# Linear attention and a feed-forward part in one kernel: last tokens of two heads in one tile, three weight differences on VectorE, stores on SyncE

## The chip, the cores and the metric

The kernel runs on one core of a Trainium2 chip, which has eight. The time is that of one execution of the whole program in device microseconds (us). A core has TensorE (PE in the profile; PEld is its weight loads), VectorE (DVE), ScalarE (ACT), GpSimd (POOL) and SyncE (SP), each with a queue of its own that it works off in order, and 16 DMA engines. A DMA is issued from the queue of SyncE, ScalarE or GpSimd.

## The reference

```python
def phi(x):
    proj = np.einsum('bhsd,df->bhsf', x, w_phi)
    proj = proj - np.max(np.abs(proj), axis=-1, keepdims=True)
    return np.concatenate([np.exp(proj), np.exp(-proj)], axis=-1)
q_p, k_p = phi(q), phi(k)                         # (8, 8, 576, 256)
kv = np.einsum('bhsf,bhsd->bhfd', k_p, v)
z = np.sum(k_p, axis=2)
num = np.einsum('bhsf,bhfd->bhsd', q_p, kv)
den = np.einsum('bhsf,bhf->bhs', q_p, z)[..., None] + 1e-06
x = (num / den).transpose(0, 2, 1, 3).reshape(4608, 512)
h = np.maximum(np.maximum(x @ w1, x @ w2), x @ w3)
return h @ w_out
```

There are 8 batches of 8 heads, 576 tokens and 64 elements a head; `w_phi` is 64 x 128, w1, w2 and w3 are 512 x 768, `w_out` is 768 x 512. Inputs and output are float32.

## The kernel before, in words

Attention runs in 16 **units**, each four heads of one batch. A unit's 576 tokens are 512 and the last 64, because a tile has 128 rows: a head has four full tiles of q and half a tile, so the half tiles are special throughout. A unit passes these stages, whose kinds are the names of nodes in the code:

- loads: `Lq` and `Lk` from GpSimd (they turn float32 into bf16), `Lv` (v) and `Lt` (the last tokens of q, `tail_raw`) from SyncE; `C` copies the last tokens beside k in `qk_bf`.
- `T` turns q and k so that the head's elements lie across the rows (`qkT`): on TensorE with a copy (`Tc`) for units 0 to 3, by a DMA transpose from SyncE for the others.
- `G` projects with `w_phi`; VectorE takes the largest absolute value (`rk`, `rq`), ScalarE the exponentials of k (`ek`); `M` projects q the other way round, with `eq` for its exponentials `Eq`.
- `E` makes the row factors `em` of k, GpSimd multiplies v by them (`va`, written to `vab`, whose last column is the factor itself, `vd`), and `K` multiplies by `Ek` (`kvps`, copied to `kv_sb`).
- `N` makes the numerators and, in column 65, the denominators: one product per tile and sign g of the exponent (`psn`). VectorE scales the one sign by `sq` (`xu`), adds the other (`xw`) and inverts the denominators (`xr`, `rden`); GpSimd divides (`x`, into `x_sb`).
- `X` turns x into `xT`: on TensorE with a copy for units 0 and 1, by a DMA transpose from SyncE for the others.

The feed-forward part runs in 9 **chunks** of 512 tokens: chunk b takes the first 512 tokens of all heads of batch b, that is the units 2b and 2b+1, and chunk 8 takes the last 64 tokens of all batches, which GpSimd gathers from `xT` (function `last`). The maximum of three products is rewritten: with the differences w2 - w1 and w3 - w1 (six nodes `wd`, each 256 columns of one matrix, made in place in `w_bf`), the kernel needs only max(0, x(w2 - w1), x(w3 - w1)), and x w1 w_out comes back as one product of x with a matrix that it makes once (`wt`, `we`, `wm`, `mo`; `lc` copies it later). So a chunk has 12 groups `up` into `ups`, evacuated by `t1` (relu) and `h` (maximum), then four groups `straight` and `down` into `ops`, a copy `osb`, and a store.

Every step is a node with its engine and the things that it waits for. **What sets the order** is a table, `PLAN`, of some 1,560 words such as `1201T4@37.6`: node, letter of the engine, buffers, and a start by which the words of one engine are put in order. Code reads the table and emits nodes in that order; on the chip an engine then goes as its semaphores let it. While n.start is below `WARM`, TensorE gets products of a constant (`idler`) in its gaps.

Of the kernel before, what the change touches and what calls it, by code (L numbers as in the profile page):

```python
# [8 lines left out]
FP32 = mybir.dt.float32  # L9
BF16 = mybir.dt.bfloat16  # L10
# [22 lines left out]
XW = SM + P  # L33
# [4 lines left out]
BY_HALF = 0  # L38
BY_BATCH = 99
# [10 lines left out]
TRAW = 2  # L50
WD_PE = 0
# [37 lines left out]
9G0@1.2 10S0@0.8 3A@1.1 1D@0.8 2G@1.9 16S0@1.3 0G@2.1 103G1@2.7 104G@7.2 4A@1.8 12D@4.0 8G@7.5 6D@4.2 11A@4.0  # L89
19T0@4.5 5A@4.3 7A@4.6 20D0@5.2 25T1@5.8 187S1@2.9 13S@4.5 26D@6.4 29T23@6.3 102G@8.2 30A0@6.7 51T45@6.9 73T67@7.1 110T0@8.0  # L90
105S1@5.1 34A0@7.2 106T1@8.1 18S2@5.7 53D0@7.3 33A@7.7 32D0@7.9 35D@8.5 107D1@9.1 119T53@9.9 75A0@8.2 31A@8.7 260G2@8.9 77A@9.1
74A0@9.6 186G3@9.6 259G@10.4 111D@9.7 76A@10.1 112T21@10.1 188G@11.1 124A1@10.6 123A1@11.1 126T06@10.3 52D@9.9 128A@11.5 17G@11.3 122D1@10.5
115D@11.1 127A@11.8 1166G@11.5 15D@11.7 27T4@12.1 14D@12.0 117A@12.1 120A@12.5 121A@13.0 1167G@12.3 1169G@13.0 130D1@12.2 28D@12.5 43T76@12.8
21T4@13.0 261G@13.8 129D@12.7 46D@13.1 47D@13.5 54A0@13.6 113A@13.8 78T0@13.3 22D@13.8 36T56@14.3 118D@14.1 125D@14.7 56G0@14.0 44A@14.3
114A@14.5 79A@15.0 23T4@14.6 39D@15.3 40A@15.3 24D@15.9 42D@16.3 48T23@16.4 55G@15.1 137A1@15.8 139G1@16.2 80A@16.0 45A@16.2 50D@16.9
116A@16.5 185G@17.3 58A@17.0 108T4@16.7 37A@17.2 334S0@11.6 140G@18.0 263T0@17.2 57A@17.7 59G@18.2 60G@19.3 267T7@17.7 68T13@17.9 61G@20.4
38A@17.8 49D@17.5 81A0@18.3 109D@18.1 264D2@18.7 268D@19.3 41A@18.5 72A@18.9 71A@19.4 138G@20.5 141A@19.9 131T25@18.8 142G@21.6 144A@20.1
62T46@19.1 64A0@20.2 69A@20.3 63A@20.8 70A@21.0 134T07@19.7 132D@19.5 190T3@20.1 65T26@20.6 1168G@22.7 133D@20.1 156T54@21.2 135D@20.7 82T01@21.6
67A@21.4 66A@21.6 161T6@21.9 136D@21.3 158A1@21.7 191D3@21.8 85T27@22.1 159A1@22.2 143G@23.4 83D0@22.4 160A@22.7 86D@22.9 333G0@24.5 157A@23.2
84D@23.3 164A1@23.7 265T3@22.6 163A@23.9 87D@23.7 332G@25.2 162A@24.1 145T04@23.4 146A1@24.4 151T21@23.9 147A@24.5 194T5@24.3 266D@24.1 155A@24.7  # L100
152A@25.2 195D@24.7 1180T7@24.4 93T60@24.8 153A@25.6 88D0@24.9 89G0@26.0 1181D0@25.0 1172G@27.6 90T34@25.1 154A@26.1 94D1@25.6 148T57@25.7 149A@26.6
91D@26.0 283T62@26.3 1178T3@26.5 165T15@27.0 285A0@26.7 284A0@27.0 95D@26.4 92D@26.8 1176T0@27.3 150A@27.3 287D0@27.2 96D1@27.5 1179A@27.4 168T47@27.7
97G@29.7 286D0@27.6 335G@30.9 196T26@28.1 98T3@28.5 166D2@28.0 1177A@28.3 169D@28.4 200A1@29.2 198A1@29.7 176T14@28.9 197A@30.1 167D@28.8 170D@29.2
276T50@29.4 177D0@29.6 99D@30.0 277A@30.6 173T71@30.1 178D@30.4 100T3@31.0 171D2@30.8 202D1@30.9 1170G@31.1 174D@31.5 278A@31.1 281A@31.6 199D@31.9
280A@32.1 175D@32.5 172G1@33.2 1186T4@31.4 1184T7@32.7 192T2@34.0 279D@32.9 210T15@34.6 179D0@33.5 403G1@34.4 337S0@38.0 189S3@39.4 101A@32.5 1187A@33.1
180G@35.1 201A@33.6 203T34@34.7 1185A@34.2 282D@33.6 208A@35.1 1171G@36.3 1173G@38.4 205A@35.6 262S0@40.0 214D1@34.9 269T60@34.9 270A@36.1 274A@36.5
181T7@35.2 1182T5@35.5 1183A@37.0 193D@35.2 183T2@36.8 473S1@40.6 182D@35.8 209D@36.2 204A@37.5 1188T7@37.1 272D@36.8 184D@37.4 213D@37.8 206D@38.1
271A@38.0 1189A@38.6 1194T5@38.4 207A@39.0 301T26@39.3 212A@39.5 275D@38.7 1175G@40.5 294A0@39.8 402G@42.6 1174G@43.3 221A1@40.0 224A0@40.2 305A0@40.3
288T37@39.6 304A0@40.8 303A@41.2 211A@41.7 1195D1@39.4 338S@42.2 336S2@43.9 297A1@42.0 1202T4@39.9 273A@42.1 302A@42.6 404G@45.4 289D@40.0 223G@45.7
612S0@45.8 290D@40.6 1200T5@40.7 1196T3@41.6 222G@47.7 1203D@41.2 291T76@42.6 228T41@42.8 229A1@43.2 1201D@41.8 1197D@42.7 230A1@43.7 218T50@43.0 293D@43.3  # L110
1206T2@43.3 238T3@44.2 1192T6@44.3 220D@43.9 232A@44.2 219D@44.5 406S1@47.4 1207D@45.1 239A@44.6 240A@44.9 1193A@45.4 215T40@45.3 306T53@45.5 292D@45.7
231A@45.8 216D@46.2 217D@46.8 1214T2@45.8 1204T6@46.7 1215D@47.4 310A@46.3 1205D@48.0 307A@46.8 309A@47.3 475S1@50.0 1198T7@47.5 241A0@47.7 339T14@48.5
# [12 lines left out]
541G@69.6 1226A3@71.3 395D@71.2 610G@70.3 386D@71.6 397D@72.0 485T64@71.8 490A1@72.2 545S2@67.5 492T03@72.0 496D1@72.4 750G2@71.0 398D@72.7 399D2@73.3
# [817 lines left out]
```

## Time and profile before

| | |
|---|---|
| median of the runs shown (3) | 281.54 us (281.24 to 284.22) |
| the profiled execution's own time | 282.56 us |
| its span, first to last instruction | 280.8 us |
| granted TensorE clock | 1.000 |
| DMA | 44.52 MB, mean 159 GB/s |
| engines, busy | PE 96%, DVE 77%, ACT 71%, POOL 58% |

A share of busy time is a mean over stages; matmuls are pipelined, so a busy TensorE is not one at its peak. Times in the rows below are microseconds from the first instruction of the span, and L with a number is a line of the kernel before.

### The profile page before, as it was taken

To read this page: it belongs to the slowest core of one execution; us is meant where nothing else is said; L and a number is where in the kernel's file an instruction comes from. 1 tells how busy PE (TensorE), PEld (TensorE's weight loads), DVE (VectorE), ACT (ScalarE), POOL (GpSimd) and SP (SyncE) were. 2 spreads that over 40 slices of the span, in tenths; PEclk is the share of its full clock that TensorE was granted. 3 is DMA by queue.
4 is the path that set the end of the run, shared out by engine and by line. 5 is a ranking of instruction groups with operands and counts; after the bars stand their busy time and mean duration, and the time that the engine had idled before them with its cause. 6 is when DMAs were issued, how large, how long until landed. Compare 5 with 4: busy or idle time off the path is not lost. (4 is left out here: it accounts for less than half of the span.)

```text
span 280.8 us, 8401 instructions
## 1 busy us (share of the span) xinstructions
PE 268.3 (96%) x3409; PEld 150.8 (54%) x3447; DVE 217.3 (77%) x442; ACT 199.1 (71%) x489; POOL 161.5 (58%) x161
## 2 busy tenths in 40 slices
PE   8789899999999999999999999999999999999993
PEld 5457654576655555555555456655546544444441
DVE  2799989999999969889997899898876871157320
ACT  4799999999999787698978879989589200310001
POOL 4879999998949703897336848393495341000000
PEclk9999999999999999999999999999999999999999
DMA  7999999997999999999999997717130224110253
GB/s 136 300 202 208 207 173 310 260 164 132 171 186 249 236 196 281 169 171 144 189 263 204 188 276 125 151 55 170 39 86 3 77 47 121 40 75 0 82 144 112
DMA packets 76214, 44.52 MB, mean 159 GB/s; under 512 B 52688, under 2 KB 67344, under 8 KB 76176
## 3 DMA queue, kind: packets, MB, share of 16 engines
q1 hardware_dynamic: 59536, 29.21, 49.8%
q0 software_dynamic: 14912, 11.77, 28.7%
q10 hardware_dynamic: 1728, 3.02, 3.0%
q8 instruction: 27, 0.44, 0.7%
q14 instruction: 11, 0.09, 0.1%
HBM read 34.64 MB, written 9.44 MB: 157 GB/s over the span
## 5 line engine op out<-in xcount | busy, mean ns | idle before, releaser
L748 PE MATMUL ups<-xT,w_bf 128*128 128x512 bf16 x414 | 101.3, 379 | 1.0
L584 ACT ACTIVATE Eq<-psm 128x512 bf16<-128x512 f32 (+1 forms) x160 | 81.7, 587 | 5.4 <-PE psm L593 3.1
L548 POOL TENSOR_TENSOR vab<-v_raw,em 128x1152 bf16<-128x1152 f32 (+1 forms) x36 | 68.2, 1907 | 22.9 <-ACT em L542 15.0
L504 ACT ACTIVATE Ek<-psk 128x512 bf16<-128x512 f32 x128 | 72.1, 633 | 8.2 <-PE psk L496 6.3
L748 PEld LDWEIGHTS <-w_bf 128*128 128x128 bf16 x432 | 39.2, 98 | 43.9 <-issue 2.3
L690 POOL TENSOR_TENSOR x_sb<-y,rden 128x640 bf16<-128x640 f32 x32 | 39.9, 1256 | 39.5 <-DVE rden L689 39.0
L786 PE MATMUL ops<-wout_bf,hT 128*128 128x512 bf16 (+2 forms) x214 | 50.5, 373 | 0.3
L758 DVE TENSOR_TENSOR hT<-hT,ups 128x512 bf16<-128x512 bf16 x54 | 35.5, 677 | 13.3 <-PE ups L748 11.1
L500 DVE TENSOR_REDUCE mq<-psq 128x4 f32<-128x512 f32 x64 | 41.2, 682 | 3.5 <-PE psq L496 3.2
L500 DVE TENSOR_REDUCE mk<-psk 128x4 f32<-128x512 f32 x64 | 41.9, 679 | 2.1 <-PE psk L496 1.7
L762 ACT ACTIVATE hT<-ups 128x512 bf16<-128x512 f32 x36 | 21.9, 620 | 24.5 <-PE ups L748 24.4
L641 DVE TENSOR_TENSOR y<-psn,sq 128x325 f32<-128x325 f32 x64 | 30.4, 491 | 6.7 <-PE psn L632 4.3
L796 ACT COPY osb<-ops 128x512 f32<-128x512 f32 x20 | 12.2, 608 | 32.3 <-PE ops L786 31.8
L786 PEld LDWEIGHTS <-hT 128*128 128x128 bf16 x222 | 20.6, 98 | 22.5 <-issue 0.2
L632 PEld LDWEIGHTS <-Eq 128*128 128x128 bf16 x640 | 26.3, 98 | 10.3 <-issue 0.4
L644 DVE TENSOR_TENSOR y<-y,psn 128x325 f32<-128x325 f32 x64 | 29.7, 487 | 1.6
L632 PE MATMUL psn<-kv_sb,Eq 128*128 128x65 bf16 x640 | 28.8, 194 | 0.2
L496 PEld LDWEIGHTS <-qkT 64*128 64x128 bf16 x576 | 18.0, 94 | 13.4 <-issue 8.3
L781 PE MATMUL ops<-xT 128*128 128x512 bf16 x87 | 23.7, 380 | 0.5
L567 PE MATMUL kvps<-vab,Ek 64*128 64x65 bf16 x1152 | 22.1, 191 | 0.8 <-POOL vab L548 0.6
L567 PEld LDWEIGHTS <-Ek 64*128 64x128 bf16 x1152 | 20.3, 94 | 3.4 <-issue 1.3
L796 DVE COPY osb<-ops 128x512 f32<-128x512 f32 (+2 forms) x17 | 11.1, 657 | 12.5 <-PE ops L786 12.5
(65 smaller groups left out, 263.9 us busy)
## 6 DMA issues: line engine op xcount, KB each, us to landing
v_raw<-in_v_dram SPq DMA_DIRECT2D x15, 576.0 KB, 6.0
out_dram<-osb SPq DMA_DIRECT2D x23, 256.0 KB, 3.3
qk_bf<-in_k_dram POOLq DMA_DIRECT2D x15, 288.0 KB, 6.9
qk_bf<-in_q_dram POOLq DMA_DIRECT2D x15, 256.0 KB, 8.7
w_bf<-in_moe_w_dram POOLq DMA_DIRECT2D x3, 768.0 KB, 13.2
out_dram<-osb ACTq DMA_DIRECT2D x9, 256.0 KB, 3.4
tail_raw<-in_q_dram SPq DMA_DIRECT2D x16, 64.0 KB, 4.8
wout_bf<-in_moe_w_out_dram POOLq DMA_DIRECT2D x1, 768.0 KB, 19.2
```

The source lines that it names most:

```text
L500: return nd(kind, {"DVE": 0.598 if n == 4 else 0.331}, lambda: nc.vector.tensor_reduce(dst(m()), ps()[:, 0:n, :], AXX, ALU.max, apply_abso ...
L504: return nd("ek", {"ACT": 0.478 if n == 4 else 0.264}, lambda: nc.scalar.activation(dst(Ek[g]()), ps()[:, 0:n, :], EXP, scale=1.0 - 2.0 * ...
L548: made.append(chosen(n_, lambda n_, g=g, t0=t0, t1=t1: (nc.vector if n_.eng == "DVE" else nc.gpsimd).tensor_tensor(vab()[:, g, t0:t1, 0:D] ...
L567: nc.tensor.matmul(kvps[ab]()[:, pr, g, :], lhsT=Ek[g]()[r, t, :], rhs=vab()[r, g, t, :], start=(pr == prs[0] and g + j == 0), stop=(pr == ...
L584: return nd("eq", {"ACT": 0.478 if n == 4 else 0.264}, lambda: nc.scalar.activation(Eq[g]()[:, t0:t0 + n, :], ps()[:, 0:n, :], EXP, scale= ...
L632: nc.tensor.matmul(psn[g]()[:, i, :], lhsT=Eq[g]()[:, t, :], rhs=kv()[:, pr, ab, g, :], start=True, stop=True)
L641: n_ = nd("xu", {"DVE": 0.064 + 0.0676 * n_t}, lambda: nc.vector.tensor_tensor(yv(y()), ps(0), sq_of(sq()).unsqueeze(len(shape) - 1).to_br ...
L644: return nd("xw", {"DVE": 0.064 + 0.0674 * n_t}, lambda: nc.vector.tensor_tensor(yv(y()), yv(y()), ps(1), ALU.add), [n_], [psn[1], y], loc ...
L690: divs[pr] = nd("x", {"POOL": 1.2}, lambda pr=pr, y=y, rden=rden: nc.gpsimd.tensor_tensor(x_sb()[:, pr].rearrange("p t a d -> p a t d"), y ...
L748: nc.tensor.matmul(ups()[:, o * n:(o + 1) * n], lhsT=w_bf[i + (not plain)][:, ct, jj * P:(jj + 1) * P], rhs=tokens_of(ct)[:, cols] if halv ...
L758: nc.vector.tensor_tensor(dst, dst, src, ALU.max)
L786: nc.tensor.matmul(ops_()[:, 0:hi - lo], lhsT=hT()[:, j, tt * P:(tt + 1) * P], rhs=wout_bf[:, j, lo:hi], start=plain and j == 0, stop=(j = ...
```

## The change

1. The half tiles. The last 64 tokens of two heads stood in one tile up to the exponentials already (heads 0 and 1, 2 and 3), but its numerators were taken once for each head, and half of each result was of no use, so that a unit had 20 tiles from `N` on. Now heads 0 and 2, 1 and 3 share a tile to the end, and a unit has 18. The exponentials of the shared tiles go to `eq_ends`, where each head's 64 columns have 64 columns of zeros beside them (set once by GpSimd, node `zero`); a shared tile's numerators are two products that add up in one place of `psn`, one for each head. The groups are three of six tiles (12, 12 and 16 products), not four of five (10 each).
2. What follows from it: `xu`, `xw`, `xr` and `x` run on 6 tiles three times a unit instead of 5 four times (and `x`, `xr` on 10 twice); `sq` takes one exponential a unit, not two; the transposes of x have 9 blocks, not 10; `xT` has another layout, and `last` has one copy a batch, not two. Each unit loads its own last tokens in two DMAs, where two units shared two DMAs of twice the size.
3. `wd` may run on VectorE: three of the six do. So may `x`, the copy of the last tokens and `va` in the first four units; one `x` and three of those copies go there, one copy to ScalarE, and no `va`.
4. `Lv` and all stores but one are issued by SyncE; ScalarE issued one and ten.
5. A new `PLAN`, whose rows tell a reader nothing. Options that were off (`BY_HALF`, `BY_BATCH`, `WD_PE`) are gone from the code, which changes no instruction.

```diff
-TRAW = 2
+TRAW = 4
...
-    xT = const.tile([P, B, CT, XW], BF16, name="xT")
+    xT = const.tile([P, B, 2, XB], BF16, name="xT")
+    eq_ends = const.tile([P, ES, 2, 2, 3, ST], BF16, name="eq_ends")
...
+            ends = q[b, h0:h0 + HU, SM:S, :].rearrange("(a r) i d -> a i r d", r=2)
+            for a in range(2):
+                queue_of[n_.eng].dma_start(t_raw()[a * ST:(a + 1) * ST], ends[a])
+        n_t = chosen(nd("Lt", {"SP": 1.24}, None, [], [t_raw], xfer=[(8, 18.0, 0.62)] * 2), load_t)
+        n_ = nd("C", {"POOL": 0.24, "DVE": 0.13, "ACT": 0.17} if by_pe else {"POOL": 0.24}, None, [n_t], [t_raw, qk_b], port=True)
...
-        main_v = chosen(nd("Lv", {"SP": 0.42, "ACT": 0.6}, None, [], [vraw], xfer=[(16, 93.0, 0.42)]),
+        main_v = chosen(nd("Lv", {"SP": 0.42}, None, [], [vraw], xfer=[(16, 93.0, 0.42)]),
...
-        eqs["t"] = [q_exp(a, psm, 2, g, NQ) for g in range(2)]
+        eqs["t"] = [nd("eq", {"ACT": 0.264}, lambda g=g: nc.scalar.activation(
+            Et()[:, g, :, 0:3:2, :], psm()[:, 0:2, :].rearrange("p r (z c) -> p r z c", z=2), EXP, scale=1.0 - 2.0 * g),
+                       [a, n_tab], [psm, Et], locks=[psm]) for g in range(2)]
...
+        n_sq = nd("S", {"ACT": 0.1}, lambda: nc.scalar.activation(sq(), mq(), EXP, scale=-2.0), reds_q, [mq, sq])
+        x_sb = buf("x_sb", XSB, [P, UT, D], BF16)
+        for th in range(3):
+            mine = range(6 * th, 6 * th + 6)
...
+                        for pr in range(2):
+                            pad = Et()[:, g, t - NQ, pr:pr + 2, :].rearrange("p z c -> p (z c)")
+                            nc.tensor.matmul(o, lhsT=pad, rhs=kv()[:, pr, t - NQ, g, :], start=(pr == 0), stop=(pr == 1))
...
+            n_ = nd("x", {"POOL": 0.767, "DVE": 0.464} if by_pe else {"POOL": 0.767}, None, [n_], [y, rden, x_sb], port=True)
...
+                nc.sync.dma_start_transpose(out=xT[:, b, u % 2, :].rearrange("p (t c) -> p t c", c=P),
+                                            in_=x_sb().rearrange("p t d -> p (t d)"))
...
-                    s_ = ff("store", {"SP": 0.41, "ACT": 0.6} if n_out == 1 else {"SP": 1.2}, None, [e], [osb],
+                    s_ = ff("store", {"SP": 0.41} if n_out == 1 else {"SP": 1.2}, None, [e], [osb],
...
-                nc.gpsimd.tensor_tensor(dst[:, :, c], dst[:, :, c], w_bf[0][:, :, c], ALU.subtract)
-            n_ = node("wd", 0, {"POOL": 2.1}, None, [w_nodes[0], w_nodes[i + 1]], [], port=True)
+                (nc.vector if n_.eng == "DVE" else nc.gpsimd).tensor_tensor(dst[:, :, c], dst[:, :, c], w_bf[0][:, :, c], ALU.subtract)
+            n_ = node("wd", 0, {"POOL": 2.1, "DVE": 0.64}, None, [w_nodes[0], w_nodes[i + 1]], [], port=True)
...
-        nc.gpsimd.tensor_copy(xT[D:P, b, :, SM:SM + ST], xT[D:P, b, :, SM + ST:XW])
-        nc.gpsimd.tensor_copy(x_last[b // 4][:, :, b % 4 * ST:(b % 4 + 1) * ST], xT[:, b, :, SM:SM + ST])
+        nc.gpsimd.tensor_copy(x_last[b // 4][:, :, b % 4 * ST:(b % 4 + 1) * ST].rearrange("p (u c) n -> p u c n", u=2),
+                              xT[:, b, :, 2 * SM:XB].rearrange("p u (c n) -> p u c n", n=ST))
```

Three places where the order moves. The first is VectorE at the very start; `k_raw` is unit 0's k, `tps` what TensorE turned, `psk` and `psq` are projections. Before:

```order
L415 CAST qk_bf<-k_raw 128x320
L337 CAST wph<-wphi_f 64x128
L472 COPY qkT<-tps 128x512 x2
L500 TENSOR_REDUCE mq<-psq 128x4
L500 TENSOR_REDUCE mk<-psk 128x4 x2
L470 COPY qkT<-tps 128x2x512
L470 COPY qkT<-tps 128x2x128
```

Now:

```order
L394 CAST qk_bf<-k_raw 128x320
L394 CAST qk_bf<-k_raw 128x256
L340 CAST wph_low<-wphi_f 64x128
L340 CAST wph<-wphi_f 64x128
L448 COPY qkT<-tps 128x512
L478 TENSOR_REDUCE mk<-psk 128x4
L394 CAST qk_bf<-k_raw 128x320
```

The copies of 128x2x512 and 128x2x128 in the first piece are unit 1's; they stood among unit 0's. Now the second half of unit 0's k (the second cast of 320) comes there, and unit 1's k follows once unit 0 is projected.

The second place is GpSimd from the first division to the time when chunk 0 begins. Before:

```order
L690 TENSOR_TENSOR x_sb<-y,rden 128x2x5x64
L844 TENSOR_TENSOR w_bf<-w_bf 128x4x256
L690 TENSOR_TENSOR x_sb<-y,rden 128x2x5x64
L430 CAST qk_bf<-tail_raw 128x2x64
L844 TENSOR_TENSOR w_bf<-w_bf 128x4x256
L690 TENSOR_TENSOR x_sb<-y,rden 128x2x5x64
L393 DMA qk_bf<-in_k_dram 128x2x576
L690 TENSOR_TENSOR x_sb<-y,rden 128x2x5x64
L844 TENSOR_TENSOR w_bf<-w_bf 128x4x256 x3
```

Now:

```order
L725 DMA w_bf<-in_moe_w_dram 128x4x768
L623 TENSOR_TENSOR x_sb<-y,rden 128x384 x3
L741 TENSOR_TENSOR w_bf<-w_bf 128x4x256
L623 TENSOR_TENSOR x_sb<-y,rden 128x384 x3
L741 TENSOR_TENSOR w_bf<-w_bf 128x4x256
L378 DMA qk_bf<-in_k_dram 128x2x576
L373 DMA qk_bf<-in_q_dram 128x4x256 x3
L741 TENSOR_TENSOR w_bf<-w_bf 128x4x256
```

Two differences, not two and then three, lie around the divisions, and the last load of a weight matrix (w2) stands just ahead of them. The other three differences are VectorE's, in this piece of its new order:

```order
L637 COPY xT<-pxT 128x384 x2
L478 TENSOR_REDUCE mq<-pst 128x2
L478 TENSOR_REDUCE mk<-pst 128x2 x2
L741 TENSOR_TENSOR w_bf<-w_bf 128x4x256 x2
L478 TENSOR_REDUCE mq<-pst 128x2
L478 TENSOR_REDUCE mk<-psk 128x4 x2
L671 TENSOR_TENSOR hT<-hT,ups 128x512
L677 TENSOR_SCALAR hT<-ups 128x512
```

Two of them use w2, and follow the last copies of units 0 and 1 into `xT`; unit 3's reductions and chunk 0's first evacuations stand behind them.

The third place is SyncE ahead of chunk 4, whose x comes from units 8 and 9. Before:

```order
L478 DMA_TRANSPOSE qkT<-qk_bf 128x10x128
L435 DMA v_raw<-in_v_dram 128x2x576
L478 DMA_TRANSPOSE qkT<-qk_bf 128x10x128
L478 DMA_TRANSPOSE qkT<-qk_bf 128x8x128
L722 DMA_TRANSPOSE xT<-x_sb 128x10x128 x2
```

Now:

```order
L711 DMA out_dram<-osb 128x512
L413 DMA v_raw<-in_v_dram 128x2x576
L454 DMA_TRANSPOSE qkT<-qk_bf 128x8x128
L454 DMA_TRANSPOSE qkT<-qk_bf 128x10x128
L641 DMA_TRANSPOSE xT<-x_sb 128x9x128
L454 DMA_TRANSPOSE qkT<-qk_bf 128x8x128
L413 DMA v_raw<-in_v_dram 128x2x576 x2
```

The transposes of units 8 and 9 stood together; now unit 8's is earlier, and unit 9's, the one in this piece, has a store, a v load and two transposes of other units straight ahead.

535 lines of the change are left out of this document (212 added, 323 removed).

## The prediction

> **What bounds the kernel now.** I read the busy times first, then a table of stretches, then who waited for whom on TensorE, and last the timeline where these pointed.
>
> ```profile
> PE 268.3 (96%) x3409; PEld 150.8 (54%) x3447; DVE 217.3 (77%) x442; ACT 199.1 (71%) x489; POOL 161.5 (58%) x161
> ```
>
> TensorE is the bound by share, but a share is a mean. Stretches of the span (busy of PE, PEld, DVE, ACT, POOL, then the granted clock, DMA share, GB/s):
>
> ```profile
> 9.40:20.00 10.60, 9.67 (x109) 6.03 (x109) 9.19 (x21) 8.70 (x26) 8.07 (x12) 1.00 1.25 230
> 20.00:40.60 20.60, 19.25 (x382) 13.76 (x383) 19.64 (x46) 20.26 (x53) 20.55 (x20) 1.00 1.20 198
> 40.60:60.00 19.40, 19.14 (x310) 10.80 (x312) 18.80 (x37) 19.01 (x52) 18.95 (x16) 1.00 1.12 252
> 60.00:100.00 40.00, 39.50 (x583) 22.72 (x590) 37.08 (x79) 37.63 (x94) 32.72 (x29) 1.00 1.09 196
> 100.00:140.00 40.00, 39.68 (x571) 22.48 (x576) 35.17 (x73) 33.58 (x82) 23.19 (x24) 1.00 1.25 187
> 140.00:160.00 20.00, 19.20 (x230) 10.37 (x233) 17.24 (x34) 17.11 (x42) 11.20 (x12) 1.00 1.19 229
> 160.00:220.00 60.00, 59.27 (x891) 34.04 (x902) 51.34 (x105) 49.56 (x123) 36.21 (x32) 1.00 0.48 108
> 220.00:276.30 56.30, 55.96 (x291) 26.35 (x294) 25.38 (x46) 7.39 (x13) 4.97 (x7) 1.00 0.26 78
> ```
>
> Chunk 0 of the feed-forward part begins at 40.8. Up to there TensorE looks busy with warming products; GpSimd (20.55 of 20.60), ScalarE and VectorE have no room. Behind it TensorE is idle for 0.26 + 0.50 + 0.32 + 0.80 + 0.73 + 0.34 = 2.95 us in all. So there are two places to win: **when chunk 0 can begin**, and those 3 us with a little spacing between matmuls that counts as busy. Two waits on TensorE have a named cause outside it:
>
> ```profile
> PE tps L459 <- DMA qk_bf<-in_k_dram: 1.6, 1, 1.6
> PE kvps L567 <- POOL vab L548: 0.6, 1, 0.6
> ```
>
> **The change, part by part.** TensorE's own work stays: a unit's numerators were 4 groups of 10 products and are now 12, 12 and 16, again 40, so this term is 0. VectorE's two passes over them and GpSimd's division shrink from 20 tiles to 18:
>
> ```profile
> L641 DVE TENSOR_TENSOR y<-psn,sq 128x325 f32<-128x325 f32 x64 | 30.4, 491 | 6.7 <-PE psn L632 4.3 <-PE psm L600 1.5 <-ACT Eq L584 0.8
> L644 DVE TENSOR_TENSOR y<-y,psn 128x325 f32<-128x325 f32 x64 | 29.7, 487 | 1.6
> L689 DVE RECIPROCAL rden<-y 128x10 f32<-128x10 f32 x32 | 6.4, 206 | 0.2
> L844 POOL TENSOR_TENSOR w_bf<-w_bf 128x1024 bf16<-128x1024 bf16 x6 | 12.6, 2121 | 0.0
> L610 ACT ACTIVATE sq<-mq 128x16 f32<-128x16 f32 (+1 forms) x32 | 5.4, 235 | 0.2 <-DVE mq L500 0.2
> ```
>
> A pass over six tiles costs at most 390 / 325 = 1.2 of one over five, 589 and 584 ns, since part of each is fixed. VectorE: 64 x 0.978 = 62.6 us becomes 48 x 1.173 = 56.3 or less; 16 more reciprocals take 3.3 of that back, so at least 3.0 us are saved before the weight differences. GpSimd loses three differences, 3 x 2.12 = 6.4 us, four casts of last tokens and one of the two copies that gather them for the last chunk. ScalarE loses 16 of the 32 short exponentials, 16 x 0.235 = 3.8 us, and nine of its ten stores. Nearly all of this lies beside TensorE's work, so it counts only where TensorE waits.
>
> Term 1, the first wait. Unit 1's transposes stood early on TensorE and waited 1.6 us for its k. They now stand behind all of unit 0's projections. What stands there instead needs the second half of unit 0's k, which SyncE issued behind four small transfers:
>
> ```profile
> 0.74 0.40 SPq L408 DMA_DIRECT2D k_raw<-in_k_dram  x1
> 1.19 2.72 SPq L426 DMA_DIRECT2D tail_raw<-in_q_dram  x4
> 3.96 0.60 SPq L408 DMA_DIRECT2D k_raw<-in_k_dram  x1
> ```
>
> It now goes second, some 2.7 us earlier. Ends: 0, if the full DMA queue only moves the wait, and -1.6. I take -1.4, near the row, since the wait's cause is gone.
>
> Term 2, the last division before chunk 0 (start, length, engine, line, operation):
>
> ```profile
> 28.09 1.27 POOL L690 TENSOR_TENSOR x_sb<-y,rden 128x640 bf16<-128x640 f32 x1
> 32.85 2.11 POOL L844 TENSOR_TENSOR w_bf<-w_bf 128x1024 bf16<-128x1024 bf16 x1
> 32.98 0.21 DVE L689 RECIPROCAL rden<-y 128x10 f32<-128x10 f32 x1
> 34.92 1.25 POOL L690 TENSOR_TENSOR x_sb<-y,rden 128x640 bf16<-128x640 f32 x1
> 35.66 0.20 DVE L689 RECIPROCAL rden<-y 128x10 f32<-128x10 f32 x1
> 36.91 1.27 POOL L690 TENSOR_TENSOR x_sb<-y,rden 128x640 bf16<-128x640 f32 x1
> 39.84 0.48 DVE L718 COPY xT<-pxT 128x640 bf16<-128x640 bf16 x1
> 40.81 1.03 PE L748 MATMUL ups<-xT,w_bf 128*128 128x512 bf16 x4
> ```
>
> The first row is unit 0's first division; the rest are unit 1's. The first of these was ready at 33.19 and began at 34.92, behind a weight difference; the second was ready at 35.86 and began at 36.91. From there the chain runs through TensorE's transpose and VectorE's copy to chunk 0. With half the differences gone from GpSimd the first could gain 1.7 and the second 1.05. VectorE is full there too, so I take -0.9; the ends are 0 and -2.6.
>
> Term 3, the wait of kvps for vab near 150. Its cause is a v load behind slow transposes in SyncE's queue:
>
> ```profile
> 140.25 0.57 SPq L435 DMA_DIRECT2D v_raw<-in_v_dram  x1
> 140.99 7.33 SPq L478 DMA_TRANSPOSE qkT<-qk_bf  x2
> 148.49 2.12 POOL L548 TENSOR_TENSOR vab<-v_raw,em 128x1152 bf16<-128x1152 f32 x1 [1.55 <-DMA v_raw<-in_v_dram]
> 148.37 3.74 SPq L722 DMA_TRANSPOSE xT<-x_sb  x2
> 156.82 1.89 PE L748 MATMUL ups<-xT,w_bf 128*128 128x512 bf16 x8
> ```
>
> The place is reordered; I take -0.6, ends 0 and -0.6. Term 4: of the other 2.35 us of idle TensorE, with the relief of VectorE and ScalarE, I take a little over half, -1.4, ends 0 and -2.35.
>
> Term 5, differences on VectorE. No row has this form; the ends for one are a copy of as many elements and GpSimd's own 2.12:
>
> ```profile
> L858 DVE COPY hT<-pwT 128x1024 bf16<-128x1024 bf16 x1 | 0.7, 692 | 0.0
> w_bf<-in_moe_w_dram POOLq DMA_DIRECT2D x3, 768.0 KB, 13.2
> ```
>
> I take 0.7, nearest in engine and type. Two of them need the matrix that is now issued last, just ahead of the first division (28.1 in this trace): 28.1 + 13.2 = 41.3, where the two stand beside chunk 0's begin, about 39.7. VectorE would wait there with unit 3's reductions and chunk 0's first evacuations behind it, and TensorE for these. Two groups of products with the other matrix stand ahead and cover part. I take +0.6; ends 0 and +3.0 (1.6 of load and 2 x 0.7).
>
> Term 6, SyncE alone. Each unit now loads its own last tokens, 16 more issues, and nine stores come over from ScalarE:
>
> ```profile
> L800 SPq DMA_DIRECT2D out_dram<-osb x32: 332/531/1148, 81.8 to 276.1; - x32
> L800 ACTq DMA_DIRECT2D out_dram<-osb x10: 338/345/1597, 86.5 to 276.9; - x10
> L478 SPq DMA_TRANSPOSE qkT<-qk_bf x24: 1242/1535/4561, 37.9 to 173.8; - x24
> DMA to landing us min/median/max: 3.3/3.6/7.2
> 69.10 1.35 SPq L722 DMA_TRANSPOSE xT<-x_sb  x1
> 75.41 1.47 PE L748 MATMUL ups<-xT,w_bf 128*128 128x512 bf16 x5
> ```
>
> The third column block is shortest, median and longest in ns; the line of landings is that of xT's transposes. A small load took 2.72 / 4 = 0.68 at the start, so 16 x 0.68 + 9 x 0.53 = 15.7 us more go through one queue. The cover: x's transpose is issued by 70.45 for chunk 1, whose products begin at 75.41, 5.0 later; by 152.11 for chunk 4 at 156.82, 4.7 later. With the median landing of 3.6 from a start 1.35 before (2.3 behind the issue) some 2.5 us are spare. Below that the added issues cost nothing. I take +0.7; ends 0 and +7.5 (below).
>
> Sum: -1.4 - 0.9 - 0.6 - 1.4 + 0.6 + 0.7 = -3.0 us. The profiled execution took 282.56 with a span of 280.8; it becomes 279.56. It was 1.02 above the median of the runs, 281.54, so the forecast for the median is **278.5 us**, faster by 1.07%.
>
> **The rivals.** *The transfers set the head.* The DMA share is 1.25 and 1.20 up to 40.6, with 230 and 198 GB/s; the bytes wanted before chunk 0 are hardly fewer. Then terms 1 and 4 come to nothing, SyncE's issues stay hidden, and 281.5 - 0.9 - 0.6 + 0.6 = 280.6. For it: the wait ended by a load. Against: chunk 0's last link is a division, not a load.
>
> *The two engines exclude each other.* If a difference on VectorE and an operation on GpSimd hold each other up, each of the two differences before chunk 0 waits up to 2.12 us, a mean of half, 1.06, and GpSimd as long as each lasts, 0.7: 278.5 + 2 x 1.06 + 2 x 0.7 = 282.0, no change. GpSimd's differences took 2110 to 2132 ns beside a full VectorE, but no VectorE operation of this trace reads two operands from SBUF, so it cannot tell.
>
> [...]
>
> *SyncE becomes the bound (slower).* One pair of tail loads (1.36), one store (0.53) and one transpose caught while the queue is full (4.56 - 1.24 = 3.3) ahead of x's transpose make 5.2 us, some 2.5 beyond what is spare, and the chunk's products wait for that. The full state holds for chunks 1 to 4, while the DMA share is above 1. At three of the four: 278.5 + 3 x 2.5 = 286.0. It decides from 2.5 us of added delay at a chunk's start. For it: term 3's rows, where this queue has already made TensorE wait. Against: the two starts shown have room, and the doubled tail loads are wanted much later than they are issued.
>
> **How the numbers follow.** Forecast 0.46, transfers 0.20, exclusion 0.16, SyncE 0.18. One per cent, 2.8 us, is about what a measurement of this kernel can tell from no change; so faster 0.46, within it 0.36, slower 0.18. The likeliest case alone spans 275 to 280. The low end for all takes the full gains of terms 1, 2 and 4, 281.5 - 1.6 - 2.6 - 2.35, or 275.0; the high end is the slow rival's 286.0.
>
> **What would show it.** Right: chunk 0's first ups begin near 38.5 to 39; no wait of tps for k; y's operations take under 0.59 us; kvps finds vab ready near 150. Wrong: chunk 0 at 40 or later; w_bf on VectorE over 1.5 us, or idle ahead of it; gaps before ups at chunks 1 to 4 ended by xT's transposes.

## The result, and the profile after

The changed kernel takes 285.84 us (median; 285.75 to 286.25), the kernel before 281.92 on the same chip: a ratio of 1.0139, 95% interval 1.0099 to 1.0178. It is slower by 1.4% where faster by 1.1% was forecast. Some executions of a kernel are a few per cent slower than its others on the same chip (e3: 284.21 to 296.44 us); medians count all of them, ratios and their intervals leave the slow ones out. The profiled execution took 285.78 us, its span is 284.0 (before 282.56 and 280.8).

The page's busy times and its row of the granted clock:

```profile
PE 269.0 (95%) x3392; PEld 153.4 (54%) x3434; DVE 221.7 (78%) x439; ACT 197.4 (70%) x468; POOL 150.3 (53%) x164
PEclk9986799999999999999999999999999999999998
```

TensorE's busy time has hardly grown (268.3 before) while the span has grown by 3.2 us, so most of the loss is idle time. The clock row says where to look: slices 3 to 5, that is 14 to 35 us. Before, no slice was under 9 there. The table of stretches, with the columns of the prediction's and without two of its stretches (from 40.6 to 60 TensorE is idle for 1.08 us, before for 0.26; from 220 to 276.3 for 0.32, before for 0.34):

```profile
9.40:20.00 10.60, 7.42 (x89) 4.39 (x87) 10.60 (x19) 9.83 (x26) 9.24 (x12) 0.95 1.15 257
20.00:40.60 20.60, 18.86 (x336) 14.49 (x334) 17.99 (x41) 15.64 (x39) 13.15 (x17) 0.78 1.22 209
60.00:100.00 40.00, 39.37 (x600) 22.88 (x605) 37.12 (x78) 38.80 (x95) 29.49 (x33) 1.00 1.16 205
100.00:140.00 40.00, 39.21 (x648) 23.23 (x653) 34.27 (x72) 36.19 (x88) 25.59 (x26) 1.00 1.14 219
140.00:160.00 20.00, 19.68 (x263) 11.19 (x266) 18.80 (x38) 17.69 (x43) 13.20 (x14) 1.00 0.99 186
160.00:220.00 60.00, 59.21 (x877) 33.88 (x885) 51.61 (x105) 48.39 (x117) 32.06 (x33) 1.00 0.62 118
```

In the first row VectorE is busy for all of 10.60 us while TensorE has fallen from 9.67 to 7.42. In the second, VectorE, ScalarE and GpSimd all have time left over, which they did not have before, and TensorE's clock averages 0.78. The waits on TensorE (some rows left out):

```profile
PE idler L804 <- DVE mq L478: 2.0, 1, 2.0
PE kvps L548 <- DVE y L616: 1.5, 1, 1.5
PE ups L662 <- DVE w_bf L741: 0.9, 1, 0.9
PE ups L662 <- DMA xT<-x_sb: 0.4, 1, 0.4
```

Both waits of before (tps for k, kvps for vab) are gone, and new ones have come, three of them on VectorE. The timeline shows what stands ahead of the first two (start, length, engine, line, operation; some rows left out):

```profile
15.90 2.29 POOL L529 TENSOR_TENSOR vab<-v_raw,em 128x576 bf16<-128x576 f32 x2
16.46 2.48 DVE L408 CAST qk_bf<-tail_raw 128x128 bf16<-128x128 f32 x1
18.11 0.81 POOL L373 DMA_DIRECT2D qk_bf<-in_q_dram  x1
18.65 0.68 DVE L478 TENSOR_REDUCE mq<-psq 128x4 f32<-128x512 f32 x1
18.93 1.17 POOL L529 TENSOR_TENSOR vab<-v_raw,em 128x576 bf16<-128x576 f32 x1
19.38 0.37 PE L804 MATMUL idler<-idle 128*128 128x256 bf16 x1 [2.05 <-DVE mq L478]
...
26.57 1.84 DVE L408 CAST qk_bf<-tail_raw 128x128 bf16<-128x128 f32 x1
27.18 1.14 POOL L529 TENSOR_TENSOR vab<-v_raw,em 128x576 bf16<-128x576 f32 x1
28.33 0.55 DVE L616 TENSOR_TENSOR y<-psn,sq 128x390 f32<-128x390 f32 x1
28.93 0.79 PE L548 MATMUL kvps<-vab,Ek 64*128 64x65 bf16 x27 [1.49 <-DVE y L616]
```

A copy of 128 columns of last tokens, which the change moved from GpSimd to VectorE, takes 2.48 and 1.84 us. The same line, grouped by engine (ns: shortest, median, longest):

```profile
L408 DVE CAST qk_bf<-tail_raw x3: 216/1839/2483, 9.7 to 26.6; 128x128 bf16<-128x128 f32 x3
L408 POOL CAST qk_bf<-tail_raw x12: 279/288/303, 26.9 to 172.7; 128x128 bf16<-128x128 f32 x12
```

The one of 216 ns, at 9.7 us, ran while GpSimd did nothing. The two long ones began while GpSimd was multiplying v, and each ended within 0.1 us of the end of a GpSimd operation: the first at 18.94, behind two products and a load, the second at 28.41, behind a product. GpSimd's work went straight on both times; between the two products of the first row VectorE got no turn. Behind each copy on VectorE stands a reduction or a product that TensorE needs, so TensorE idles; with each of these two stretches of idleness (2.05 and 1.49 us) its clock went to 0.50 for some microseconds (18.9 to 25.7 and 29.2 to 32.6). Chunk 0's first products of x begin at 44.2 instead of 40.8.

### The profile page after: what moved, and what is told of

Same layout as the page of the kernel before. It is cut to its first block, busy times and chain, and to the rows that moved or that the text cites. A ratio compares the mean times of both kernels' runs of the same rounds, so it can differ in the third digit from the quotient of the medians.

```text
span 284.0 us, 8364 instructions
## 1 busy us (share of the span) xinstructions
PE 269.0 (95%) x3392; PEld 153.4 (54%) x3434; DVE 221.7 (78%) x439; ACT 197.4 (70%) x468; POOL 150.3 (53%) x164
## 4 chain that ended last, share of the span: by engine, by line
PE 76%; DVE 10%; DMA 5%; ACT 3%; issue 3%; POOL 1%; SPq 0%; POOLq 0%; DVEq 0%; ACTq 0%
PE ups L662 29%; PE ops L699 14%; PE ops L694 11%; PE kvps L548 6%; PE psn L605 5%; DMA v_raw<-in_v_dram 3%; PE psk L474 3%; DVE mk L478 3%; PE psm L574 2%; PE psq L474 2%; DVE mq L478 2%; DVE qk_bf L408 2%; DMA xT<-x_sb 1%; ACT Eq L565 1%; DMA k_raw<-in_k_dram 1%
## 5 line engine op out<-in xcount | busy, mean ns | idle before, releaser
L662 PE MATMUL ups<-xT,w_bf 128*128 128x512 bf16 x410 | 99.7, 379 | 2.4 <-DVE w_bf L741 0.9
L565 ACT ACTIVATE Eq<-psm 128x512 bf16<-128x512 f32 x128 | 71.1, 627 | 4.1 <-PE psm L574 4.0
L623 POOL TENSOR_TENSOR x_sb<-y,rden 128x384 bf16<-128x384 f32 x47 | 38.1, 825 | 31.7 <-DVE rden L621 31.4
L707 ACT COPY osb<-ops 128x512 f32<-128x512 f32 (+2 forms) x25 | 15.1, 607 | 34.7 <-PE ops L699 18.2
L675 ACT ACTIVATE hT<-ups 128x512 bf16<-128x512 f32 x32 | 19.3, 622 | 23.5 <-PE ups L662 17.3
L616 DVE TENSOR_TENSOR y<-psn,sq 128x390 f32<-128x390 f32 x48 | 26.3, 556 | 6.2 <-PE psn L605 4.2
L619 DVE TENSOR_TENSOR y<-y,psn 128x390 f32<-128x390 f32 x48 | 25.9, 554 | 2.1
L605 PEld LDWEIGHTS <-Eq 128*128 128x128 bf16 x512 | 21.4, 99 | 7.3 <-issue 0.4
L605 PE MATMUL psn<-kv_sb,Eq 128*128 128x65 bf16 x512 | 23.4, 195 | 0.1
L677 DVE TENSOR_SCALAR hT<-ups 128x512 bf16<-128x512 f32 x22 | 14.9, 683 | 7.7 <-PE ups L662 7.3
```

The source lines that it names most:

```text
L565: return nd("eq", {"ACT": 0.478 if n == 4 else 0.264}, lambda: nc.scalar.activation(Eq[g]()[:, t0:t0 + n, :], ps()[:, 0:n, :], EXP, scale= ...
L605: nc.tensor.matmul(o, lhsT=Eq[g]()[:, 8 * (c % 2) + 4 * pr + 2 * ab + c // 2, :], rhs=kv()[:, pr, ab, g, :], start=True, stop=True)
L623: divs.append(chosen(n_, lambda n_, th=th, y=y, rden=rden: (nc.vector if n_.eng == "DVE" else nc.gpsimd).tensor_tensor(x_sb()[:, 6 * th:6 ...
L662: nc.tensor.matmul(ups(), lhsT=w_bf[i + (not plain)][:, ct, j * P:(j + 1) * P], rhs=tokens_of(ct), start=(ct == 0), stop=(ct == CT - 1))
```

## The experiments

Theory A: VectorE's copy of last tokens is shut out by GpSimd, and this with its consequences is the loss. Rivals: SyncE's queue, now alone with all stores and loads; the weight differences on VectorE; the low clock as a cause of its own. A word of the order table is an operation's number, its engine (D VectorE, A ScalarE, G GpSimd, S SyncE) and its planned time.

**e1_casts_scalar.** The two copies go to ScalarE at the same places:

```
-192D@16.4   +192A@16.4
-265D@23.1   +265A@23.1
```

> The two copies of last tokens of units 2 and 3 (VectorE took 2.48 and 1.84 us for them, 0.22 for unit 1's) go to ScalarE, which takes 0.29 us for one; nothing else moves. Theory A (VectorE is shut out by GpSimd's operations during such a copy, and TensorE, starved by it, is granted half its clock): both copies' delays and both stretches of half clock go, chunk 0's first ups begin near 38.5 instead of 44.2, and the time falls by 5 to 7 us to 279 to 281. Theory B (SyncE's longer queue costs the time): within 1 us of 285.8. Theory C (the head is set by the transfers): the wait only moves, 284 to 286.

Measured: 280.89 us, ratio to the kernel before 0.9941 (0.9904 to 0.9978). Two words of the table bring back 5 us and turn the loss into a gain. Its stretches and the rows around chunk 0:

```profile
9.40:20.00 10.60, 9.08 (x132) 5.70 (x127) 10.25 (x20) 10.58 (x30) 9.33 (x12) 1.00 1.15 254
20.00:40.60 20.60, 19.75 (x344) 13.64 (x342) 19.35 (x48) 20.14 (x50) 18.14 (x22) 1.00 1.24 206
60.00:100.00 40.00, 39.95 (x602) 22.70 (x600) 36.81 (x74) 38.83 (x95) 28.23 (x29) 1.00 1.14 205
100.00:140.00 40.00, 39.70 (x580) 22.54 (x579) 35.15 (x74) 35.67 (x88) 27.84 (x29) 1.00 1.15 214
140.00:160.00 20.00, 20.00 (x342) 11.87 (x339) 18.59 (x39) 17.47 (x41) 10.19 (x12) 1.00 1.07 183
160.00:220.00 60.00, 60.00 (x826) 33.74 (x825) 51.64 (x105) 43.85 (x107) 34.21 (x37) 1.00 0.52 113
...
38.84 1.89 PE L662 MATMUL ups<-xT,w_bf 128*128 128x512 bf16 x8
39.59 2.25 POOL L373 DMA_DIRECT2D qk_bf<-in_q_dram  x3
39.70 2.74 DVE L741 TENSOR_TENSOR w_bf<-w_bf 128x1024 bf16<-128x1024 bf16 x2
41.89 2.76 PE L662 MATMUL ups<-xT,w_bf 128*128 128x512 bf16 x12 [1.16 <-DVE w_bf L741]
```

In this profile the clock stays at 1.00. Chunk 0 begins at 38.84, 2 us ahead of the kernel before, and then loses 1.16 us to a weight difference.

**e2_casts_as_reductions.** The copies stay on VectorE, in the same places, in another form: a maximum over an axis of length one.

```
+            if n_.eng == "DVE" and u in (2, 3):
+                nc.vector.tensor_reduce(dst, t_raw().unsqueeze(3), AXX, ALU.max)
+            else:
+                copy_on[n_.eng](dst, t_raw())
```

> The same two copies stay on VectorE at their places, but as a maximum over an axis of one element, so the data and the waits are the same and the form of the operation is another. Theory A, if it is the form of the copy that is shut out: each takes 0.2 to 0.3 us and the time is that of the run with ScalarE within 1 us, 279 to 281. If any VectorE operation with both sides in SBUF is shut out: 1.8 us or more each, and 285 to 286. Theory B: 285 to 286 whatever they take.

Measured: 281.46 us, ratio 0.9928 (0.988 to 0.9975). The two reductions, on the same data (the first ran beside two of GpSimd's products, 16.36 to 18.63, the second while GpSimd issued a load):

```profile
L411 DVE TENSOR_REDUCE qk_bf<-tail_raw x2: 275/276/277, 16.9 to 23.8; 128x128 bf16<-128x128 f32 x2
```

So neither the engine nor the data is shut out, but this form of the operation: 2.48 us as a copy, 0.28 as a reduction.

**e3_stores_scalar.** Nine stores go back to ScalarE (nine words S to A).

> Nine of the stores go back to ScalarE, in the chunks in which it issued them before the change. Theory A: SyncE does not set the time, 285.3 to 286.5. Theory B: 2 us or more are won, below 284.

Measured: ratio 1.0128 (1.0077 to 1.018), as the changed kernel. The copies again took 2.41 and 2.51 us. SyncE's stores aren't the loss.

**e4_warm_gap.** Sixteen more warming products are put where TensorE idled first:

```
+                if 16.4 < t < 16.6:
+                    todo += [(t, make(best[1])) for _ in range(16)]
```

> Sixteen more warming products stand on TensorE just ahead of the first gap (17.3 to 19.4), so that it is busy for most of it; VectorE's copies stay as they are. Theory A with the clock as a cost of its own: the granted clock stays at 1.0 through 19 to 25, the first stretch of half speed costs nothing and the time falls by 0.8 to 1.5 us to 284.3 to 285.0. If the half clock costs nothing because other engines set the pace there: 285.5 to 286.2, and the warming products change only the clock.

Measured: 292.26 us, ratio 1.0229 (1.0147 to 1.031): worse than without them. From the profile, of an execution that took 296.22 us: the products (first row) and the clock (stretch, its length, TensorE's busy time, clock, DMA share, GB/s):

```profile
17.09 6.16 PE L806 MATMUL idler<-idle 128*128 128x256 bf16 x17
...
19.00:20.00 1.00, 0.81 (x3) 1.00 1.15 209
21.00:22.00 1.00, 0.86 (x3) 0.50 1.21 205
```

I had counted 0.11 us for each; they came 0.33 us apart, so they filled 6 us instead of 2 and stood in the way. And the clock fell although the profile, which models the ends of products, shows TensorE over 0.8 busy, with three short products in a microsecond; why it fell was not shown. This run can't price the clock.

**e5_copies_scalar_differences_gpsimd.** e1 with the three differences of VectorE back on GpSimd (1169D, 1167D and 1171D become G).

> The changed kernel with its two copies of last tokens on ScalarE (as in e1_casts_scalar, 280.9 us) and all six differences of weights on GpSimd again, as before the change. Theory A (VectorE's operation on two operands in SBUF is held up while GpSimd runs its own or issues DMAs; the differences lose about 1.3 us in e1, where the first took 2.14 us and TensorE waited 1.2 us for it): GpSimd alone needs 3 x 2.1 us one after the other from 38.9 us, so the first difference is ready at about 41.0, the second at 43.1, the third at 45.2, against 41.8, 42.4 and 44.4 in e1: the wait for the first shrinks by 0.8 us and the later ones grow by about as much, time 280 to 281.5. Rival B (work on VectorE is worth its price in any case, since GpSimd is three times slower at a difference): over 1.5 us slower than e1, 282.5 or more.

Measured: 284.94 us, ratio 1.0086 (1.0058 to 1.0115), 4 us slower than e1: rival B, and I was wrong. TensorE waited twice:

```profile
PE ups L662 <- POOL w_bf L741: 3.6, 2, 1.8
```

With chunk 0 ready at 38.9, GpSimd's 2.1 us for each difference, with the loads between them, are too slow. The move to VectorE pays, even with the stall that it meets.

**e6_before_one_copy_on_vector.** The kernel before, with unit 2's copy moved to VectorE (188G@11.1 becomes 188D@16.6).

> The kernel before with one thing changed: unit 2's copy of last tokens is moved from GpSimd, which does it before its first products of v, to VectorE, at the place in the order where GpSimd is in the middle of those products (about 16 us). Theory A (the copy form is shut out by GpSimd's running instructions): the copy takes 1.5 to 3.5 us where it takes 0.22 to 0.29 alone, the reductions behind it are late, TensorE idles 1 to 3 us there, and the time grows by 1.5 to 5 us (284 to 287), the more the lower granted clock follows. Rival (the copy was slow in the changed kernel for its data or its layout, four heads' tail in two pieces, or because transfers were late): about 0.3 us and no change, 281.5 to 282.5.

Measured: 282.98 us, ratio 1.002 (0.9985 to 1.0055): no loss, where theory A expected 1.5 us or more.

```profile
L430 DVE CAST qk_bf<-tail_raw x1: 587/587/587, 18.5 to 18.5; 128x128 bf16<-128x128 f32 x1
```

VectorE reached it only at 18.48, in the last of three products of GpSimd (15.61 to 18.98), and it ended with that product: 0.59 us where it takes 0.22 alone. The copy was held up, but only by what was left of GpSimd's products, so this run neither supports a price of 1.5 us nor rules it out. That the price depends on how much of GpSimd's run is still to come is my reading here; e12 below bears on it.

**e7_forms_beside_gpsimd** measures forms by themselves.

> Computes nothing of the reference: a kernel that measures the disputed costs by themselves. VectorE runs eight forms one at a time, each with GpSimd idle, then beside two products of GpSimd (128x576 fp32 to bf16, as for v), then beside three of its DMA issues: a copy fp32 to bf16 of 128x128, a reduction over an axis of length one of the same data, a copy fp32 to fp32, a copy bf16 to bf16 of 128x1024, a difference of bf16 of 128x1024, a copy from PSUM, a product of PSUM and SBUF, a reduction from PSUM. Beside it TensorE runs stretches of 40 products of 128x512 with gaps between them made by ScalarE, of about 0.5, 0.9, 1.5, 2 and 2.5 us. Theory A: beside GpSimd the three copies in SBUF and the difference take about as long as GpSimd's work that is left (2 us and more), the reductions and the forms that read PSUM their own time (0.3 to 0.7 us). Rival: all forms are slowed alike, or only those with two operands in SBUF. For the clock: theory A is that a gap of 2 us is followed by 6 us at 0.50, and a gap of under 1 us isn't; rival: the low clock has another cause than idle time, and all stretches run alike.

Inconclusive: VectorE's work ran in another order than meant, so most forms met another cover. A copy of 128x1024 bf16 took 0.41 us beside nothing and 2.74 across two products; reductions and forms that read PSUM kept their time; TensorE kept its clock at 1.00 through gaps up to 2.53 us.

**e8_copies_scalar_loads_moved.** e1 with the order table changed around the differences:

```
-335G@38.3 542G2@39.0 1167D@39.2 1168G@40.5
+335G@33.95 542G2@48.3 1167G@40.3 1168D@39.8
```

> e1_casts_scalar (280.9 us) with VectorE's differences kept clear of GpSimd's DMA issues: of the three loads of q that GpSimd issued at 39.6 to 41.8 us one goes ahead to 34 us, where GpSimd waits, and one behind to 48 us; the second difference goes to GpSimd and the third to VectorE. Theory A: VectorE's first difference, which waits at 39.7 us, ends at about 40.4 instead of 41.8, TensorE's wait of 1.2 us for it goes, the second is ready at 42.5 and the third at 43.1: 0.8 to 1.3 us faster than e1, 279.6 to 280.1. Rival (the difference is late because of its late load of weights, which lands at 38.7, or TensorE's wait moves to the next chunk): as e1 within 0.4 us.

Measured: 283.6 us, ratio 1.0012 (0.9976 to 1.0049): worse than e1. All three differences on VectorE now met GpSimd's work: the first difference met two loads, the second GpSimd's own difference, the third a product:

```profile
L741 DVE TENSOR_TENSOR w_bf<-w_bf x3: 1774/2381/2599, 40.3 to 49.6; 128x1024 bf16<-128x1024 bf16 x3
```

**e9_differences_alone.** e1, but GpSimd waits until VectorE's first two differences are made, and its loads of q and k come behind its own:

```
+nc.gpsimd.tensor_copy(seen, w_bf[1][:, 0, 0:1])   # ahead of GpSimd's difference of w2
-405G1@37.6 335G@38.3 542G2@39.0 404G@39.8
+405G1@41.0 335G@41.2 542G2@48.3 404G@45.45
```

> e1_casts_scalar (280.9 us) with VectorE's first two differences of weights made while GpSimd does nothing: GpSimd's own third difference is held back by a one-column copy of their result (about 0.3 us), and its four loads come behind that difference. Theory A: VectorE's two differences start at about 39.7 us and take 0.68 us each, so the second is ready at about 41.1 instead of 42.4, TensorE's wait of 1.2 us for the first shrinks to under 0.5, GpSimd's third is ready at about 43.5 instead of 44.4, and the time falls by 0.7 to 1.2 us against e1: 279.5 to 280.3, a ratio to the kernel before of about 0.990. Rival (the differences aren't late because of GpSimd, or the loads that are moved behind are missed instead, as in e8_copies_scalar_loads_moved): no gain, 281 or more, with waits for vab or for unit 4's q after 45 us.

Measured: 284.69 us, ratio 1.0076 (1.0051 to 1.0101). The part that was aimed at did what theory A says: two differences in 1.28 us, and TensorE ran 20 products without the wait. Then the third difference met GpSimd:

```profile
39.14 4.48 PE L664 MATMUL ups<-xT,w_bf 128*128 128x512 bf16 x20
40.00 1.28 DVE L745 TENSOR_TENSOR w_bf<-w_bf 128x1024 bf16<-128x1024 bf16 x2
...
45.77 2.15 POOL L531 TENSOR_TENSOR vab<-v_raw,em 128x1152 bf16<-128x1152 f32 x1
46.65 5.40 DVE L745 TENSOR_TENSOR w_bf<-w_bf 128x1024 bf16<-128x1024 bf16 x1
48.00 0.81 POOL L375 DMA_DIRECT2D qk_bf<-in_q_dram  x1
48.83 2.14 POOL L531 TENSOR_TENSOR vab<-v_raw,em 128x1152 bf16<-128x1152 f32 x1
51.13 1.55 POOL L375 DMA_DIRECT2D qk_bf<-in_q_dram  x2
...
PE ups L664 <- DVE mq L480: 3.8, 1, 3.8
```

0.68 us of work took 5.40: VectorE got no turn through GpSimd's product, small copy, load, second product and second copy (50.90 to 51.19, not shown), and ended beside the loads behind them. In e1 the same difference came at 47.69, just as GpSimd went from one operation to the next, and took 0.68; GpSimd's product behind it took 2.62 instead of 2.11. So the hold-up goes both ways.

**e11_three_differences_alone.** e9 with the third difference behind the other two (1171D@45.5 becomes @39.8; GpSimd waits for that one).

> e9_differences_alone (284.7 us) with VectorE's third difference of weights made right behind the other two, while GpSimd still waits, in place of 46.7 us, where it took 5.40 us beside GpSimd's products of v and loads and TensorE waited 3.8 us. Theory A: three differences of 0.68 us from 40.0 to 42.0 us; TensorE's 20 products from 39.1 to 43.6 us run as in e9 without a wait, the wait of 3.8 us and the half clock behind it (51 to 59 us, some 3 us more) go, GpSimd's third difference and loads come 0.7 us later: 279 to 280.3 us, 1 us faster than e1_casts_scalar, a ratio to the kernel before of 0.987 to 0.992. Rival (a stall moves on to the next place, here vab or unit 4's q, 0.7 us later than in e9): 281 to 283.

Measured: 287.02 us, ratio 1.0199 (1.0157 to 1.0242). All three took 0.68 us, and yet the rival's mechanism came true, 4 us beyond its range of 281 to 283: the loads that stand behind them are missed elsewhere.

```profile
PE ups L664 <- DMA xT<-x_sb: 3.7, 1, 3.7
50.10 2.17 SPq L456 DMA_TRANSPOSE qkT<-qk_bf  x1
```

In e1 SyncE issued this transpose, for which q must have landed, at 45.66. What stands behind it in SyncE's queue is 2 to 5 us later here, x's first two transposes by 3.5 and 2.4; one of these is what TensorE waits for. So e1 and e2 stay the fastest.

**e10_forms_beside_gpsimd_in_order** and **e12_turns_beside_gpsimd** measure the disputed cost with every engine's order fixed.

> As e7_forms_beside_gpsimd (it computes nothing of the reference), with the order of each engine's work fixed, so that each form of VectorE meets what it is meant to meet: GpSimd idle, two products of GpSimd (2.3 us), or three DMA issues (2.3 us). Theory A: the copy fp32 to bf16 takes 0.22 us alone and 1.5 to 2.4 us beside either; the copy fp32 to fp32 and the copy bf16 to bf16 likewise; the difference of bf16 with two operands in SBUF 0.68 alone and 2 us or more beside the products; the reductions 0.28 and 0.67 and the forms that read PSUM (0.28, 0.55) their own time everywhere. Rival: a DMA issue holds up nothing by itself (in e7 three differences beside three issues took 0.68 us each). For the clock: stretches of TensorE work at full activity with gaps of 0.6, 2.5 and 4.7 us, and stretches of short products (64 columns, weights loaded each time) with gaps of 2.5 and 1.3 us. [...] Rival: low clock has nothing to do with idle time, and all run at 1.00.

> Computes nothing of the reference. VectorE's copy (fp32 to bf16, 128x128, 0.22 us alone) and its difference (bf16, 128x1024, two operands in SBUF, 0.68 us alone) are started during unbroken runs of GpSimd: four products (4.5 us); product, two small copies, product, DMA issue; four DMA issues; product, issue, product, copy, issue, product; difference, two issues, difference. Each once at once, and once 0.7 us later. Theory A, strict form (VectorE gets no turn between GpSimd's instructions while GpSimd has work): every time is that until the end of the run or until its last product, 2 to 5 us. Rival 1 (one turn at each end of an instruction, as beside two products in e10_forms_beside_gpsimd_in_order, 0.74 and 1.13 us): at most 1.2 us beside products, 2.2 beside a difference. Rival 2 (issues hold nothing up): 0.22 and 0.68 us beside four issues.

Each form's time in us (e10):

| form on VectorE | GpSimd idle | two products | three DMA issues |
|---|---|---|---|
| copy fp32 to bf16, 128x128 | 0.22 | 0.74 | 0.22 |
| copy fp32 to fp32, 128x128 | 0.22 | 0.66 | 0.22 |
| copy bf16, 128x1024 | 0.42 | 0.86 | 0.42 |
| difference bf16, 128x1024 | 0.68 | 1.13 | 0.68 |
| reduction in SBUF, 128x128 | 0.28 | 0.28 | 0.28 |
| copy from PSUM | 0.28 | 0.28 | 0.28 |
| product of PSUM and SBUF | 0.55 | 0.55 | 0.55 |
| reduction from PSUM | 0.68 | 0.68 | 0.68 |

Of these eight forms, exactly the copies within SBUF and the difference of two SBUF operands are held up, by 0.44 to 0.52 us. GpSimd pays too: its two products take 2.71 us beside the difference and 2.26 beside a reduction. Here VectorE got in after the first product. In e12 that was a matter of the moment: the difference beside four products took 1.55 us started at once and 4.16 started 0.7 us later, until the end of the run.

```profile
57.12 4.94 POOL L74 TENSOR_TENSOR vb<-va,em 128x576 bf16<-128x576 f32 x4
57.28 1.55 DVE L60 TENSOR_TENSOR d_tt_bf_TTTT<-wa,wb 128x1024 bf16<-128x1024 bf16 x1
62.14 4.47 POOL L74 TENSOR_TENSOR vb<-va,em 128x576 bf16<-128x576 f32 x4
63.01 4.16 DVE L60 TENSOR_TENSOR d_tt_bf_TTTT<-wa,wb 128x1024 bf16<-128x1024 bf16 x1
```

So rival 1 holds in part: the turn came at the end of the first product in one case (1.55) and only at the end of the last in the other (4.16). The copy, in the run of product, two small copies and product, got in at the first end (1.08) or only at the last (1.84). Rival 2 holds: four issues in a row held up nothing (0.22 and 0.68).

For the clock (e10, TensorE; the bracket is the gap ahead):

```profile
28.20 0.19 PE L90 MATMUL acc<-slow,lhs 128*128 128x64 bf16 x1 [2.52 <-ACT slow L100]
28.23 8.79 PE L92 MATMUL acc<-rhs,lhs 128*128 128x512 bf16 x40
41.76 0.21 PE L90 MATMUL acc<-slow,lhs 128*128 128x64 bf16 x1 [4.73 <-ACT slow L100]
41.79 11.27 PE L92 MATMUL acc<-rhs,lhs 128*128 128x512 bf16 x40
```

After a gap of 2.52 us, 40 products take 8.79 us at full clock; after 4.73 us they take 11.27, at 0.50 from 40.0 to 46.8. The gaps behind 80 short products, 2.52 and 1.66, changed nothing: the 40 products after each took 8.79 again. A gap of 2.52 us by itself did not halve the clock here; in the kernel one of 2.05 came among sparse work: the five microseconds before the drop at 19 were busy 0.68, 0.69, 0.76, 0.33 and 0.

## Why the prediction was wrong, point by point

**Term 1, right.** The wait of tps for k is gone, and GpSimd's first product of v begins 1.1 us earlier (14.64, before 15.75).

**Term 2, right, and hidden.** With the copies out of the way chunk 0 begins at 38.84, as "near 38.5 to 39" said: 2.0 us earlier for terms 1 and 2, forecast 2.3; what each gave was not measured apart. In the changed kernel itself it begins at 44.2, behind the stalls.

**Term 3, right.** Kvps finds vab ready: no such row is left in the waits, and in e1 TensorE is busy for 20.00 of 20 us from 140 to 160.

**Term 4, right only without the copies.** In e1 TensorE is idle for 0.05 + 0.30 + 0 + 0 = 0.35 us from 60 to 220, before for 2.35, term 3's wait among them: 2.0 us for terms 3 and 4, as forecast (0.6 + 1.4). In the changed kernel it is 0.63 + 0.79 + 0.32 + 0.79 = 2.53, no gain. That a head which ends over 3 us late upsets the order behind it is my reading and was not tried apart. The lighter operations are as forecast:

```profile
L616 DVE TENSOR_TENSOR y<-psn,sq 128x390 f32<-128x390 f32 x48 | 26.3, 556 | 6.2 <-PE psn L605 4.2 <-ACT sq L590 1.2 <-PE psn L610 0.4
```

**Term 5, the mechanism half right, the size too small.** A difference takes 0.68 us, as taken, when it is alone. "Over 1.5 us" was the sign of wrong, and one took 2.05 in the changed kernel and 2.14 in e1. TensorE waited 0.9 and 1.16 us against a forecast of 0.6, inside the ends. The reason given, the late load, is not the one: the weights had landed at 38.7 in e1, a microsecond before the difference began, and in e9, with the weights no earlier but GpSimd still, two took 1.28 us together.

**Term 6, near nothing.** TensorE's one wait for x's transpose is 0.4 us against 0.7, and e3 gains nothing. The slow rival had the sign right and the mechanism wrong, so that its 286.0 lies next to the measured 285.84 is chance; e11 shows that it exists, once something delays the head of that queue by 4 us.

**The step that failed is the price of the copies of last tokens on VectorE, which was put at nothing.** The two that meet GpSimd's work were in no term: the prediction noted only what GpSimd saves. The rival of the two engines that exclude each other, given a chance of 0.16, had the mechanism, but it priced the differences alone, which read two operands from SBUF, at 3.5 us. The copies read one, and they are what cost 5 us (e1 against the changed kernel): they took 2.48 and 1.84 us where 0.22 is their time alone, and TensorE waited for what stood behind them. Without them the forecast's sign is right and its size about half: e1 is faster by 0.6%, forecast was 1.07%. The table of e10 has both, form by form: beside two products a copy within SBUF goes from 0.22 to 0.74 us as the difference goes from 0.68 to 1.13, and a reduction stays at 0.28.

Two more things were missing in the size. Half a run of GpSimd, 1.06 us, was taken for a wait; it can be several instructions (2.48, 5.40). And lateness in the head came with a lower clock: it was at 0.50 for 6.8 and 3.4 us after the two stalls. What this share of the loss is wasn't settled, since e4 failed; e1 removes stalls and low clock together. The single executions speak against a large share: of the twelve of e9, the six with a mean granted clock of 0.981 to 0.985 took 284.00 to 285.81 us, the six with 0.991 to 0.994 took 284.14 to 285.42. No execution of the changed kernel was without the low clock (0.978 to 0.986), so for it this isn't shown.

What stays open: why VectorE is sometimes passed over at the end of an instruction; why the first difference in the kernel ended only with the last of three DMA issues (e1, 39.70 to 41.84; the changed kernel, 44.93 to 46.98), when issues by themselves held up nothing; and why the profiles of e5, e9 and e11 show half clock for 3.4 us between 17.4 and 21.4 without a long wait there, while that of e1 does not.

## What to carry to other kernels

Before an operation is moved to VectorE, ask of its form whether it copies within SBUF or reads two SBUF operands, and what GpSimd is doing then: beside a long run of GpSimd its price can be the rest of that run, not its own time (4.16 us for 0.68 in e12), and it holds everything queued behind it (TensorE waited 2.05 us in the changed kernel). Put it on ScalarE (0.29 to 0.43 us in e1), read from PSUM (0.28 in e10), or write the copy as a reduction (0.28 in e2); two words of an order table were worth 5 us here. And price small moves too: the term left out was an operation of 0.2 us, while the large ones were right.

## What the hardware showed that was not expected

- A copy of 0.22 us took 2.48, the same data as a reduction 0.28, at the same place in the order.
- VectorE can be passed over through several operations of GpSimd in a row: 0.68 us of work took 5.40 (e9) and 4.16 (e12).
- Every stretch of half clock given here lasts 3.4 us or twice that: 18.92 to 25.74 and 29.15 to 32.57 in the changed kernel, 17.44 to 20.86 in e9, 39.97 to 46.80 in e10.
- TensorE's clock fell to 0.50 with a busy share over 0.8, where the busy time was short products 0.33 us apart (e4), and did not fall after a gap of 2.52 us between dense stretches (e10). It fell 2.95 us after the last product in e10, in the gap of 4.73, and 1.6 us after it in the changed kernel, where the time before was only partly idle.
